# The order of exponentials and maxima in the fifteen sections with nine products: one order for both halves

## The chip, the cores and the metric

One core of a Trainium2 chip. The metric is device time in microseconds (us) of one execution, the median of three runs. The engines are called as in the profile: PE is TensorE (PEld its weight loads), DVE is VectorE, ACT is ScalarE, POOL is GpSimd, and SP issues most DMAs.

## The reference

```python
x = A_x                                                # 2048 x 512
g = _sigmoid((x * gate_w).sum(-1, keepdims=True))
a = einsum("ts,se->te", dft_seq_re, x @ dft_hid_re.T) - einsum("ts,se->te", dft_seq_im, x @ dft_hid_im.T)
qkv = x @ wqkv                                         # 32 heads of 16
p = softmax(q @ k.T * 16 ** -0.5)                      # for each head, 2048 x 2048
b = (p @ v, heads side by side) @ wo
out = g * a + (1 - g) * b
```

So there is an attention of 32 heads without a mask, and beside it a Fourier mixing by dense matrices; a gate mixes the two.

## The kernel before

Heads are taken in 16 pairs. A **unit** is one pair, one half of the queries (1024) and 128 keys; there are 512 units (`UNITS`). For each unit four score tiles of 128 keys x 512 queries are made: two query blocks `qb`, two heads `h`. Each is one matmul of 64 rows into one of seven PSUM banks (`scores`, L795), and one exponential on ACT that writes a quarter of the unit's tile `pt` (L796). Four `pt` tiles exist at a time. The softmax needs the maximum of each row ahead of the exponentials; for that the same products are made a second time with queries and keys exchanged, each reduced by a maximum on DVE (`a_tile`, L257 and L259), and the negated maximum goes into spare rows of the queries.

The **values** (`pv`, L831) multiply `pt` with the values of its 128 keys: for each unit four fp32 matmuls, j = 2 qb + h, each in 32 columns of the PE array of its own; the profile shows two records for each. Two units are added up in one bank, and ACT copies it (L840, or L837 for the first of a row of units); POOL adds the copies up (L846).

PE's array is split into two halves of 64 rows, so that two matmuls run side by side. What runs side by side is written out by hand as a **pattern** of slots. A letter is a score tile: "s" one that ends in an exponential, "a" one that ends in a maximum. A slot of one letter runs one dense product (`issue`, L472) on one half of the array beside a score on the other half. A slot of two letters runs two scores side by side, the first letter on the other half, the capital on the same half as the products. "d" is a dense product alone, "^" issues a small piece of deferred work of the maxima, and "|" ends the **segment**: what finishes a chain of products, the planned loads, then the values of the next two units. Scores come from two streams for each kind, one for each head h (`streams`); stream h lies on half h of the array. Segment `half` takes its products from half `half` of the array, its single letters from stream `1 - half`, its capitals from stream `half`.

A section is a pair of segments, half 0 and half 1, for the same products. Twelve sections (THIN) make the Fourier's first products, 96 (FULL) its second ones, one (EVEN) and then fifteen (TEN) the attention's output projection: nine products make one chain for 128 rows of the output, in the one bank `d`. The second half of a chain waits for the first score's reader after the last product of the segment before (`before`); the first half of the next one waits for the bank's reader, a scaling and adding on DVE (`finish`, L664), which is held back until the end of half 1 (`late`). Before all sections the routine `four` runs with four phases, and in each of them stream 0 is given one score tile ahead (`first_tiles`).

Which of the seven banks a tile gets is a plan: `bank()` takes the one that a small model of DVE's and ACT's queues (`read_by`: 2.6 slots a maximum, 2.1 an exponential) sees free first. PE, ACT, DVE and POOL each work through their instructions in the order of the program; semaphores hold what isn't ready.

Of the kernel before, what the change touches and what calls it, by code (L numbers as in the profile page):

```python
# [32 lines left out]
def mix_kernel(ctx: ExitStack, tc: tile.TileContext, xa_t, xa, wqkv, w_hid, w_seq, wo, gate_w, out):  # L33
# [821 lines left out]
    def take(gen, n, whole=True):  # L855

        got = []
        while len(got) < n:
            x = next(gen, None)
            if x is None:  # L860
                break
            x[0].left -= 1
            got.append((*x, x[0].left == 0))
            if whole and got[-1][4]:
                break
        return got
# [71 lines left out]
    FULL = "a s a s a s a s s a s a s a a s |"  # L938
    THIN = "aS s a s a s s a s a s a a sA |"
    EVEN = "aA s s a s ^ s d s sA a d sS |", "a s a sS a ^ s a s s s s a |"  # L940
    TEN = "aA s s a s ^ s s s a a sS |", "a s a sS a ^ s s s s s aA |"

    def stream(h):

# [74 lines left out]
    def pairs():  # L1019
# [3 lines left out]
        for i in range(2 * NT * 3):  # L1023
            yield (FULL,) * 2, take(seq, 16)
        for patterns, n in ((EVEN, 1), (TEN, 15)):
            for i in range(n):
# [83 lines left out]
```

## Time and profile before

| | |
|---|---|
| median of 3 runs | 1653.67 us (1653.55 to 1653.82) |
| the profiled execution | 1653.87 us, span 1651.8 us |
| PE, DVE, ACT, POOL busy | 99%, 82%, 77%, 46% of the span |
| the stretch of the fifteen sections, 1458.4 to 1601.5 us | ACT 137.41, DVE 108.04, POOL 46.86 of 143.10 us |
| one section | 8 + 8 exponentials, 2 copies, 10 maxima, 9 + 9 products |

The span goes from the first to the last instruction. A row of the timeline gives start and duration of consecutive instructions of one kind, their count, and in brackets the engine's idle time before them with what ended it. A row of the groups gives the count, the busy time, the mean of one in ns, and the idle time before them. PE's matmuls are pipelined: the duration of one is longer than its distance from the next.

### The profile page before, as it was taken

The page shows a single profiled execution, that of the slowest core. Times are in us where ns is not written, and L with a number is a line of the kernel's source. Part 1 is how long each engine was busy: PE and PEld are TensorE (multiplying, and loading weights), DVE is VectorE, ACT ScalarE, POOL GpSimd, SP SyncE. Part 2 cuts the span into 40 slices and gives each one's busy share as a digit, 9 for nine tenths or more (in the row PEclk, how much of TensorE's full clock was granted, in tenths as well). Part 3 has the DMA queues.
Part 4 walks back from the last instruction along what each step waited for, and adds up shares of the span by engine and source line. Part 5 has one row for each costly group of instructions (what it writes and reads, how often), then busy time and mean ns, then how long its engine had stood idle before and what let it go on. Part 6 is the DMA issues. An engine that isn't in the chain of part 4 may idle for free.

```text
span 1651.8 us, 35235 instructions
## 1 busy us (share of the span) xinstructions
PE 1643.1 (99%) x13169; PEld 1012.2 (61%) x13169; DVE 1356.4 (82%) x2285; ACT 1267.7 (77%) x2487; POOL 753.0 (46%) x813
## 2 busy tenths in 40 slices
PE   9999999999999999999999999999999999999998
PEld 7888866665555665565555555555555555555554
DVE  5469988888888888888888888888888888877776
ACT  5222178888888888888887888888888888899995
POOL 0124644554544555545454565554545566332341
PEclk9999999999999999999999999999999999999999
DMA  9953301112221234222227333322222333451114
GB/s 302 340 162 135 154 14 37 31 53 66 67 71 52 61 87 133 74 62 70 57 75 259 84 95 114 96 77 68 66 72 74 81 114 109 151 197 43 24 44 142
DMA packets 92481, 165.66 MB, mean 100 GB/s; under 512 B 23360, under 2 KB 24776, under 8 KB 91160
## 3 DMA queue, kind: packets, MB, share of 16 engines
q1 hardware_dynamic: 87672, 162.64, 32.2%
q8 instruction: 104, 1.70, 0.4%
q0 software_dynamic: 4352, 0.39, 0.2%
q14 instruction: 65, 0.53, 0.1%
q10 hardware_dynamic: 288, 0.39, 0.1%
HBM read 107.73 MB, written 54.52 MB: 98 GB/s over the span
## 4 chain that ended last, share of the span: by engine, by line
PE 99%; DVE 0%; DMA 0%; SPq 0%; DVEq 0%; ACT 0%; issue 0%
PE d L472 44%; PE t L831 28%; PE t L257 8%; PE t L795 6%; PE t L353 5%; PE t L92 2%; PE t L93 2%; PE t L91 2%; PE t L812 1%; PE t L472 1%; PE t L377 1%; DMA raw<-xa_t 0%; DVE mx L259 0%; DVE yp L664 0%; PE t L749 0%; PE t L727 0%
## 5 line engine op out<-in xcount | busy, mean ns | idle before, releaser
L259 DVE TENSOR_REDUCE mx<-t 128x1 f32<-128x512 f32 x2009 | 1232.6, 681 | 225.5 <-PE t L257 206.1
L796 ACT ACTIVATE pt<-t 128x512 f32<-128x512 f32 x2048 | 1031.1, 629 | 11.4 <-PE t L795 3.2
L257 PE MATMUL t<-ks,qs 64*128 64x512 f32 x2009 | 750.2, 407 | 0.1
L795 PE MATMUL t<-qs,ks 64*128 64x512 f32 x2048 | 729.2, 394 | 0.2
L472 PE MATMUL d<-xab,ch 64*128 64x512 f32 x2016 | 647.2, 396 | 0.0
L831 PE MATMUL t<-pt,vt 128*32 128x512 f32 x3968 | 477.2, 598 | 0.0
L472 PEld LDWEIGHTS d<-xab,ch 64*128 64x128 f32 x2016 | 366.9, 184 | 169.3 <-issue 99.7
L472 PE MATMUL d<-xab,cl 64*128 64x512 f32 x1008 | 399.2, 396 | 0.0
L257 PEld LDWEIGHTS t<-ks,qs 64*128 64x128 f32 x2009 | 357.8, 184 | 56.9 <-ACT pt L796 25.2
L795 PEld LDWEIGHTS t<-qs,ks 64*128 64x128 f32 x2048 | 367.9, 184 | 16.3 <-ACT pt L796 5.8
L846 POOL TENSOR_TENSOR osum<-osum,oe 128x512 f32<-128x512 f32 x217 | 279.1, 1286 | 157.6 <-ACT oe L840 155.8
L840 ACT COPY oe<-t 128x512 f32<-128x512 f32 x217 | 127.4, 587 | 187.2 <-PE t L831 179.0
L831 PEld LDWEIGHTS t<-pt,vt 128*32 128x32 f32 x3968 | 103.6, 109 | 223.8 <-issue 149.1
L472 PEld LDWEIGHTS d<-xab,cl 64*128 64x128 f32 x1008 | 185.8, 184 | 86.3 <-issue 49.4
L417 POOL CAST ch<-craw 128x512 fp32r<-128x512 f32 x126 | 77.2, 613 | 343.1 <-PE t L257 232.4
L418 POOL TENSOR_TENSOR cl<-craw,ch 128x512 fp32r<-128x512 f32 x126 | 162.1, 1286 | 10.2
L280 POOL DMA_DIRECT2D qs<-mt x132 | 73.5, 562 | 80.7 <-DVE mt L276 71.2
L472 PE MATMUL d<-wo_hl,o_hl 64*128 64x512 f32 x288 | 75.6, 395 | 0.0
L472 PE MATMUL d<-wre,xab 64*128 64x512 f32 x288 | 70.5, 390 | 0.0
L472 PEld LDWEIGHTS d<-wo_hl,o_hl 64*128 64x128 f32 x288 | 51.8, 184 | 18.5 <-ACT pt L796 13.4
L472 PEld LDWEIGHTS d<-wre,xab 64*128 64x128 f32 x288 | 52.8, 185 | 2.9
L92 PE MATMUL t<-xab,wh 128*128 128x512 f32 x124 | 48.4, 390 | 0.2 <-DVE xab L88 0.2
(123 smaller groups left out, 938.3 us busy)
## 6 DMA issues: line engine op xcount, KB each, us to landing
craw<-w_seq SPq DMA_DIRECT2D x128, 256.0 KB
qk<-hl SPq DMA_DIRECT2D x32, 512.0 KB
qs<-qk SPq DMA_DIRECT2D x84, 128.0 KB
ks<-qk SPq DMA_DIRECT2D x288, 32.0 KB
b<-hl SPq DMA_DIRECT2D x16, 512.0 KB
xab<-b SPq DMA_DIRECT2D x16, 512.0 KB
o<-osum SPq DMA_DIRECT2D x62, 128.0 KB
oh<-nh SPq DMA_DIRECT2D x12, 512.0 KB
```

Source lines behind the costliest of these rows:

```text
L92: nc.tensor.matmul(ps, sh, ml, start=False, stop=False)
L257: nc.tensor.matmul(ps, qs[p % 2][r, qt * P:(qt + 1) * P], ks[p % 2][r, kb * 512:(kb + 1) * 512], start=True, stop=True)
L259: user = nc.vector.tensor_reduce(mx[p % 2][:, h, qt, kb:kb + 1], ps, AX.X, ALU.max)
L353: i = nc.tensor.matmul(ps[c], st[r], mv[r], start=phase < 2 and j == 0, stop=phase > 1 and j == 11)
L417: nc.gpsimd.tensor_copy(h1, raw)
L418: nc.gpsimd.tensor_tensor(l1, raw, h1.bitcast(F32), ALU.subtract)
L472: i = nc.tensor.matmul(self.ps, st[r], mv[r], start=not self.begun, stop=stop)
L795: nc.tensor.matmul(ps, ks[p % 2][rr, kt * P:(kt + 1) * P], qs[p % 2][rr, q0:q0 + 512], start=True, stop=True)
L796: return nc.scalar.activation(pts[u][:, 2 * qb + h], ps, AF.Exp, bias=0.0, scale=DH ** -0.5)
L831: nc.tensor.matmul(acc[32 * j:32 * j + 32], vt[:, kt, p, h:h + 32], pt[:, j], start=u == us[0], stop=u == us[-1])
L840: nc.scalar.copy(oe, acc)
L846: nc.gpsimd.tensor_tensor(o, o, oe, ALU.add)
```

## The change

Both segments of the fifteen sections get the same pattern. It begins with a slot that pairs an exponential's tile with a maximum's, goes on with nine products beside s, a, s, a, s, s, a, s, a, and ends with two exponentials' tiles side by side. Each segment's count of each letter on each stream stays: seven s and four a from the far stream, one S and one A from the near one.

```diff
-    TEN = "aA s s a s ^ s s s a a sS |", "a s a sS a ^ s s s s s aA |"
+    TEN = ("sA s a s a ^ s s a s a sS |",) * 2
```

## The prediction

> **What bounds the kernel now.** I read the page first, then the granted clock and busy times of the stretch that the change touches, then that stretch's groups, then one section instruction by instruction.
>
> ```profile
> span 1651.8 us, 35235 instructions
> PE 1643.1 (99%) x13169; PEld 1012.2 (61%) x13169; DVE 1356.4 (82%) x2285; ACT 1267.7 (77%) x2487; POOL 753.0 (46%) x813
> ```
>
> By the page PE (TensorE) is the bound. That is an average, and a PE that holds a matmul in flight counts as busy. The fifteen sections with nine products lie between 1458.4 and 1601.5 us. The busy times of that stretch, and its groups:
>
> ```profile
> core 0: us, PE busy (x) PEld busy (x) DVE busy (x) ACT busy (x) POOL busy (x), PEclk, DMA share, GB/s
> 1458.40:1601.50 143.10, 143.10 (x1138) 78.84 (x1134) 108.04 (x177) 137.41 (x270) 46.86 (x48) 1.00 0.17 52
> ```
> ```profile
> L796 ACT ACTIVATE pt<-t 128x512 f32<-128x512 f32 x240 | 120.8, 628 | 0.8
> L840 ACT COPY oe<-t 128x512 f32<-128x512 f32 x27 | 15.8, 587 | 5.0 <-PE t L831 3.4
> ```
>
> Here ACT (ScalarE) works 137.41 of 143.10 us: 240 exponentials and 30 copies of the values' bank (27 of them in the second row). Nearly all its idle time, 5.0 us, stands before those copies. So ACT sets the pace, and the one thing it waits for is the end of the values' matmuls (L831). One section on ACT's timeline (start, duration, group, idle before):
>
> ```profile
> 1506.40 4.03 ACT L796 ACTIVATE pt<-t 128x512 f32<-128x512 f32 x8
> 1510.57 0.59 ACT L840 COPY oe<-t 128x512 f32<-128x512 f32 x1
> 1511.15 4.03 ACT L796 ACTIVATE pt<-t 128x512 f32<-128x512 f32 x8
> 1515.36 0.58 ACT L840 COPY oe<-t 128x512 f32<-128x512 f32 x1 [0.18 <-PE t L831]
> 1515.96 4.03 ACT L796 ACTIVATE pt<-t 128x512 f32<-128x512 f32 x8
> ```
>
> Eight exponentials, a copy, eight, a copy: half 0 then half 1. From 1506.40 to 1515.96 a section takes 9.56 us. The eight end 4.03 us after their start; their mean is 0.628, so they follow each other by (4.03 - 0.628) / 7 = 0.486. ACT then idles 1510.57 - 1510.43 = 0.14 us before the copy of half 0 and 1515.36 - 1515.18 = 0.18 before that of half 1. The loads of the values' weights and the first matmuls of each half show what PE does:
>
> ```profile
> 1505.59 0.50 PE L257 MATMUL t<-ks,qs 64*128 64x512 f32 x2
> ...
> 1508.52 0.16 PEld L831 LDWEIGHTS t<-pt,vt 128*32 128x32 f32 x8 [0.27 <-ACT pt L796]
> 1508.52 1.92 PE L831 MATMUL t<-pt,vt 128*32 128x512 f32 x16
> 1508.98 0.13 PEld L831 LDWEIGHTS t<-pt,vt 128*32 128x32 f32 x4 [0.30 <-issue]
> 1509.41 0.13 PEld L831 LDWEIGHTS t<-pt,vt 128*32 128x32 f32 x4 [0.30 <-issue]
> ...
> 1510.38 0.50 PE L257 MATMUL t<-ks,qs 64*128 64x512 f32 x1
> ...
> 1513.31 0.16 PEld L831 LDWEIGHTS t<-pt,vt 128*32 128x32 f32 x8 [0.25 <-ACT pt L796]
> 1513.77 0.13 PEld L831 LDWEIGHTS t<-pt,vt 128*32 128x32 f32 x4 [0.30 <-issue]
> 1514.20 0.13 PEld L831 LDWEIGHTS t<-pt,vt 128*32 128x32 f32 x4 [0.30 <-issue]
> 1515.17 0.50 PE L257 MATMUL t<-ks,qs 64*128 64x512 f32 x2
> ...
> 1515.51 0.38 PE L472 MATMUL d<-wo_hl,o_hl 64*128 64x512 f32 x1
> ```
>
> The values' sixteen instructions (eight matmuls, two records each) run in four waves of four, at 1508.52, 1508.98, 1509.41 and, one step of 0.43 later, 1509.84. Their start waits for an exponential. Which one can be worked out: the fourth of half 0 ends at 1506.40 + 3 x 0.486 + 0.628 = 1508.49, which is 0.03 before the waves; the fourth of half 1 ends at 1511.15 + 1.458 + 0.628 = 1513.24, 0.07 before them. So in both halves the values follow the **fourth** of eight exponentials, the last four run beside the waves, and the copy finds the waves only 0.14 to 0.18 us late.
>
> **The change part by part.** *Counts.* A half keeps 11 slots, 9 products, 8 exponentials and 5 maxima; each half still gives the far stream seven exponentials and four maxima and the near one one of each; "^" stays after the fifth slot. So streams, chains, plan and DMAs stand where they stood at every segment's end, and only the order inside a segment moves. Work added or removed: none, 0 us.
>
> *Which exponential the values need.* Counting `next()` on the streams: stream 0 was given four scores by the four row groups' phases before the sections, stream 1 none, and every section gives both eight. With V units valued, a section starts with stream 0 at 2V+4 tiles and stream 1 at 2V. Half 0 values units V and V+1, so it needs stream 1 up to 2V+4: its first four exponentials, now as before the first four on ACT. Half 1 values V+2 and V+3 and needs both streams up to 2V+8. Stream 0 stands at 2V+5 and brings three with its first three exponentials. Stream 1 got seven in half 0 and lacks one, unit V+3, query half 1, head 1. Only the capital S of half 1 brings it. Before, that S is in slot "sS", the fourth of half 1, and is the third of ACT's eight. After, it sits in the last slot and is **the eighth**. Its matmul is j = 3 of the second unit, the last of the values.
>
> *Price of that wait.* PE works in order through sixteen instructions; the first two waves can run early, but the third wave's last member waits for the eighth exponential, and its second record runs a wave later. From the third wave to the copy it is 1510.57 - 1509.41 = 1.16 us (1515.36 - 1514.20 gives 1.16 again), and a wave follows its exponential by 0.03 to 0.07. ACT, whose next instruction is that copy, then idles 1.19 to 1.23 us instead of 0.18: 1.01 to 1.05 more, taken as 1.03. Queued behind the waiting matmul on PE are all slots of the next half 0; behind the copy on ACT are that half's eight exponentials. Nothing covers it: ACT has no other work and its exponentials are the bound. 15 sections x 1.03 = 15.4 us. The cost can't be below nothing, since the eight exponentials were already done without a gap. If only the last record had to run after it, it would be one step of 0.43 less, 15 x 0.60 = 9.0; the two records per matmul speak for two waves, so I keep 15.4.
>
> The row shows eight weight loads at once, those of the second wave already beside the first wave's matmuls, so loads do run ahead of matmuls and one could hope that PE works past the waiting one. The Trainium skill, "TensorE: Matmul & The Clock Gate", section "The mechanism", says that matmuls start and end strictly in program order, and only weight loads are pulled ahead; by it nothing of the next half fills the gap and the sum stays, while a PE that worked past it would give about no loss. No run here shows that order at a wait in mid-group.
>
> *The first slot.* An exponential now comes at once instead of after a maximum's slot. ACT is at its copy then (1510.57 to 1511.15, first slot at 1510.38), so its next exponential starts no earlier: 0 us.
>
> *Maxima.*
>
> ```profile
> 1506.12 3.19 DVE L259 TENSOR_REDUCE mx<-t 128x1 f32<-128x512 f32 x5 [0.43 <-PE t L257]
> 1510.94 1.89 DVE L259 TENSOR_REDUCE mx<-t 128x1 f32<-128x512 f32 x3 [1.63 <-PE t L257]
> ...
> 1514.52 0.74 DVE L664 SCALAR_TENSOR_TENSOR yp<-d,omg,yp 128x512 f32<-128x512 f32 x1
> ```
>
> Five take 3.19 us, 0.64 each, beside eight exponentials of 4.03. Half 1 no longer ends in two maxima, so the finish of a chain (0.74) starts earlier on DVE: 0.5 + 3.19 + 0.74 = 4.4 us after the half's first matmul, before its eighth exponential ends (in half 0 that was 1510.43 - 1505.59 = 4.84 after it). The next half 0's first product waits on it through bank d and finds it done. Before, the finish was over at 1515.26 and the product started at 1515.51, so nothing is won either.
>
> *Banks.* Seven banks serve a segment's 13 tiles, so the values' bank is the seventh one that comes free. By the planner's costs (2.1 slots an exponential, 2.6 a maximum) it is the fourth exponential's in both orders. The last S takes the third maximum's. On the chip that maximum ends, in half 0, 0.53 (1506.12 - 1505.59) + 3 x 0.64 = 2.45 us after the first slot; the fourth exponential ends 1508.49 - 1505.59 = 2.90 after it. The cover is 0.45 less the slot of that S, about a quarter microsecond by PE's pace (11 slots from 1505.59 to the wait before 1508.52). So half 0 keeps its 0.14 us of idle: 0 us. If the cover failed, a values' start could be late by up to one maximum, 0.64.
>
> Sum: 1653.87 us (the profiled execution, span 1651.8 and 2.1 around it) + 15.4 = 1669.3; on the median of 1653.67, which is 0.2 lower, **1669.1 us**.
>
> **The rivals.**
>
> *All of the values wait.* Never before does an instruction inside the sixteen carry a wait of its own; if the wait came to stand at their head, four waves would follow the eighth exponential: 1510.57 - 1508.52 + 0.05 - 0.18 = 1.92 per section, 28.8 in all, 1682.5 us. For it: that the trace has no example of a wait in the middle. Against: the fourth exponential released the head until now, and the code asks for each quarter of the tile apart. 6%.
>
> *The maxima's banks.* If the third maximum came later than reckoned, half 0's values would start late too: between nothing and 15 x 0.64 = 9.6 more, up to 1678.7. It decides once that maximum ends 0.2 us later than above. Speaking for it: only 0.2 us of cover; against: DVE now gets its second maximum two slots after the first, in place of two in one slot, and is not behind. 7%.
>
> *Not slower: the late S isn't what ends the wait.* If the streams were one tile further ahead than I count, half 1's values would still need only the first four, and an order that feeds ACT from the first slot could at best remove the idle before the copies: 15 x (0.14 + 0.18) = 4.8 us, 1648.9. It decides if the third wave of half 1 starts before the eighth exponential ends. For it: the trace before can't tell data from bank, since the fourth exponential frees both. Against: the count, and that every older pattern has this S in the first four slots of half 1. 5%, of which 3% stays within 0.2%.
>
> *The clock.* PE will stand still for about 1 us in each section. A gap that dropped the granted clock would stretch PE's 4.6 us (1505.59 to 1510.44 less a wait of 0.27) of the next half. At half speed that is 4.6 us more, of which the wait of 0.3 takes up a part: 4.3 in each of 15 sections, beside what is forecast, 1734 us.
>
> ```profile
> 1642.50:1646.50 4.00, 2.23 (x18) 1.06 (x16) 3.28 (x9) 1.52 (x3) 2.48 (x3) 1.00 0.34 133
> ```
>
> In the last microseconds PE works 2.23 of 4.00 us, and the clock granted is 1.00. 2%. The Trainium skill, same page, section "A second HAM failure mode: psum-queue depth-cycling", says that short idle times between groups of matmuls that cycle through banks can make the gate swing between half and full clock; by it this would be the outcome, and the row just quoted shows none of it.
>
> **How the numbers follow.** Forecast 80%, rivals 6, 7, 5 and 2%. The range takes the bounds of the unknown costs: below, a single wave behind the late exponential, 1653.67 + 9.0 = 1662.7; above, half a maximum's delay in half 0, 1669.1 + 15 x 0.32 = 1673.9. That is 1662.7 to 1673.9, and leaves out some 15%. A measurement of this kernel can tell about 0.2%, 3.3 us: faster 2%, same 3%, slower 95%.
>
> **What would show it right or wrong.** Right: on ACT's timeline every second copy has an idle time of about 1.2 us before it, released by L831, and the others keep about 0.14; sections last 10.6 us; the values' loads of half 1 show a wait on an exponential in their middle, with two waves after it; the group L840 has about 20 us of idle time instead of 5.0; the clock in the stretch is 1.00. Wrong: both copies of a section late (banks), an idle time of 2.1 us (all values wait), 0.7 us (one wave), or no more than 0.18.

## The result, and the profile after

The changed kernel takes 1667.7 us (median of 5, 1667.55 to 1667.81) against 1653.82 of the kernel before on the same chip: a ratio of 1.0083, interval 1.0071 to 1.0094, or 13.9 us slower. The profiled execution's span is 1665.7 us, 13.9 more than before. The prediction said 1669.1 us (1662.7 to 1673.9), slower, with 80% on a late capital S in half 1.

The page's head, and the busy times of the stretch with the fifteen sections (this window runs to the end of the last copy, 157.7 us; the one of before, 143.1 us, ended about 1 us ahead of it):

```profile
span 1665.7 us, 35222 instructions
...
1458.60:1616.30 157.70, 157.70 (x1144) 83.87 (x1142) 106.46 (x179) 135.51 (x271) 47.77 (x52) 1.00 0.16 47
```

The engines do the same work as before, the granted clock (the last but two) is 1.00, and ACT's share of the stretch has fallen from 96 to 86%. ACT's timeline for one section, with the copy before it:

```profile
1510.71 0.59 ACT L840 COPY oe<-t 128x512 f32<-128x512 f32 x1 [1.19 <-PE t L831]
1511.19 4.03 ACT L796 ACTIVATE pt<-t 128x512 f32<-128x512 f32 x8
1515.53 0.59 ACT L840 COPY oe<-t 128x512 f32<-128x512 f32 x1 [0.30 <-PE t L831]
1516.01 4.03 ACT L796 ACTIVATE pt<-t 128x512 f32<-128x512 f32 x8
1521.23 0.58 ACT L840 COPY oe<-t 128x512 f32<-128x512 f32 x1 [1.19 <-PE t L831]
1521.71 0.61 ACT L796 ACTIVATE pt<-t 128x512 f32<-128x512 f32 x1
```

A section has grown from 9.56 to 1521.71 - 1511.19 = 10.52 us. Before every copy that ends half 1, ACT idles 1.19 us in place of 0.18; all fifteen rows of this kind say 1.19. The loads of the values' weights and PE's matmuls around them show why:

```profile
1510.55 0.50 PE L795 MATMUL t<-qs,ks 64*128 64x512 f32 x1
...
1513.02 0.53 PE L795 MATMUL t<-qs,ks 64*128 64x512 f32 x2
1513.48 0.16 PEld L831 LDWEIGHTS t<-pt,vt 128*32 128x32 f32 x8 [0.24 <-ACT pt L796]
...
1515.33 0.50 PE L795 MATMUL t<-qs,ks 64*128 64x512 f32 x1
...
1517.82 0.53 PE L795 MATMUL t<-qs,ks 64*128 64x512 f32 x2
1518.27 0.16 PEld L831 LDWEIGHTS t<-pt,vt 128*32 128x32 f32 x8 [0.25 <-ACT pt L796]
1518.73 0.12 PEld L831 LDWEIGHTS t<-pt,vt 128*32 128x32 f32 x3 [0.30 <-issue]
1519.16 0.12 PEld L831 LDWEIGHTS t<-pt,vt 128*32 128x32 f32 x3 [0.31 <-issue]
1520.09 0.14 PEld L831 LDWEIGHTS t<-pt,vt 128*32 128x32 f32 x2 [0.81 <-ACT pt L796]
1521.07 0.49 PE L795 MATMUL t<-qs,ks 64*128 64x512 f32 x1
```

In half 1 the values' sixteen records no longer run as four waves of four. Eight loads, then three, then three: fourteen records run on time. The last two, both of the fourth quarter of the second unit, wait until 1520.09. The eighth exponential ends at 1516.01 + 4.03 = 1520.04. The next half starts 0.98 later.

Half 0, from its first slot to the next half's, takes 1515.33 - 1510.55 = 4.78 us (before 4.79). Half 1 takes 1521.07 - 1515.33 = 5.74 (before 4.79). The loss is in half 1, 0.95 a section. Added up from copy to copy, from the last one ahead of the sections to the last one in them, the stretch was 1602.04 - 1457.88 = 144.16 us and is 1615.82 - 1458.17 = 157.65: 13.5 us more, and the other 0.4 of the 13.9 lie outside the sections. Eleven sections lose 0.95 on average. The three with a copy L837 lose 0.83, as they were a little longer before (9.64 in place of 9.56). The last loses 0.54: in the kernel before, its copy of half 0 was once 0.57 late in place of 0.14 (the row below), and after the change it is as late as the others, 0.30.

```profile
1597.27 0.59 ACT L840 COPY oe<-t 128x512 f32<-128x512 f32 x1 [0.57 <-PE t L831]
```

### The profile page after: what moved, and what is told of

Read it like the earlier page. It is cut to its first block, busy times and chain, and to the rows that moved or that the text cites. A ratio compares the mean times of both kernels' runs of the same rounds, so it can differ in the third digit from the quotient of the medians.

```text
span 1665.7 us, 35222 instructions
## 1 busy us (share of the span) xinstructions
PE 1656.9 (99%) x13169; PEld 1016.3 (61%) x13169; DVE 1353.8 (81%) x2285; ACT 1264.8 (76%) x2487; POOL 752.8 (45%) x813
## 4 chain that ended last, share of the span: by engine, by line
PE 99%; DVE 0%; DMA 0%; DVEq 0%; SPq 0%; issue 0%
PE d L472 43%; PE t L831 28%; PE t L257 8%; PE t L795 7%; PE t L353 5%; PE t L93 2%; PE t L92 2%; PE t L91 2%; PE t L812 1%; PE t L472 1%; PE t L377 1%; DVE mx L259 0%; DMA raw<-wqkv 0%; PE t L192 0%; DVE yp L664 0%; PE t L749 0%
## 5 line engine op out<-in xcount | busy, mean ns | idle before, releaser
L257 PE MATMUL t<-ks,qs 64*128 64x512 f32 x2009 | 761.4, 404 | 0.1
L795 PE MATMUL t<-qs,ks 64*128 64x512 f32 x2048 | 744.2, 396 | 0.2
L831 PE MATMUL t<-pt,vt 128*32 128x512 f32 x3968 | 491.2, 598 | 0.0
L257 PEld LDWEIGHTS t<-ks,qs 64*128 64x128 f32 x2009 | 362.2, 184 | 42.5 <-ACT pt L796 10.2
L472 PE MATMUL d<-wo_hl,o_hl 64*128 64x512 f32 x288 | 71.6, 389 | 0.0
```

The source lines that it names most:

```text
L257: nc.tensor.matmul(ps, qs[p % 2][r, qt * P:(qt + 1) * P], ks[p % 2][r, kb * 512:(kb + 1) * 512], start=True, stop=True)
L472: i = nc.tensor.matmul(self.ps, st[r], mv[r], start=not self.begun, stop=stop)
L795: nc.tensor.matmul(ps, ks[p % 2][rr, kt * P:(kt + 1) * P], qs[p % 2][rr, q0:q0 + 512], start=True, stop=True)
L831: nc.tensor.matmul(acc[32 * j:32 * j + 32], vt[:, kt, p, h:h + 32], pt[:, j], start=u == us[0], stop=u == us[-1])
```

## The experiments

Theory: the values of half 1 need the tile that the capital S brings; the change makes it the eighth exponential, and the last quarter of the values with its two records waits for it. Rival one: the mixed order of exponentials and maxima costs something by itself. Rival two: the hand-over from ACT to PE has a fixed price, or the whole block of values waits. "Slower" and "faster" below are against runs of the kernel before on the same chip.

**The late S in the old order.**

```diff
-    "a s a sS a ^ s s s s s aA |"
+    "a s a sA a ^ s s s s s aS |"
```

> The old patterns with one swap in half 1: the capital S of the fourth slot and the capital A of the last slot change places, so that only the late S is new. Theory (the values of half 1 wait for this S, now the eighth exponential): exponentials start 0.6 us after the copy as before, so the eighth ends 4.8 us after the half's first slot; 0.05 and two waves (0.98) behind it the next half begins, 5.84 in place of 4.79. 15 x 1.05 = 15.7 us slower than before, about 1.5 us slower than the change itself, whose exponentials start 0.1 earlier. Rival (the mixed order of the two kinds costs, not the S): the old order is kept, so within 2 us of before.

Measured: 1668.89 us against 1653.91, ratio 1.009 (1.0075 to 1.0105), 15.0 us slower. One exchange of two capitals makes all of the loss. It makes 1.1 us more than the change; the two intervals overlap, but the rows show where that comes from. ACT's rows for the end of half 1, half 0 and the end of the next half 1:

```profile
1510.71 0.59 ACT L840 COPY oe<-t 128x512 f32<-128x512 f32 x1 [1.19 <-PE t L831]
1511.33 4.03 ACT L796 ACTIVATE pt<-t 128x512 f32<-128x512 f32 x8
1515.50 0.59 ACT L840 COPY oe<-t 128x512 f32<-128x512 f32 x1
1516.09 4.03 ACT L796 ACTIVATE pt<-t 128x512 f32<-128x512 f32 x8
1521.30 0.58 ACT L840 COPY oe<-t 128x512 f32<-128x512 f32 x1 [1.19 <-PE t L831]
```

The idle time is the same 1.19. The exponentials start 0.59 to 0.62 us after the start of their copy, where the change has 0.48: that is its small gain, 0.1 a half, and half 1 keeps it.

**Half 0 alone.** TEN is the new pattern for half 0 and the old one for half 1.

> The new pattern in half 0 alone, half 1 as before. Theory: half 0 was 4.79 us and is 4.78 in the changed kernel, and half 1 gets its S early again: within 1 us of before. Rival (the mixed order costs): half of the loss, some 7 us.

Measured: 1653.77 against 1653.91, ratio 0.9999 (0.999 to 1.0009). The new order in half 0 costs nothing and brings nothing.

**The same order, one tile of lead.**

```diff
-    EVEN = ..., "a s a sS a ^ s a s s s s a |"
+    EVEN = ..., "a s a sS a ^ s a s s s s aS |"
```

> The changed kernel, with the same order of slots in all fifteen sections, but stream 1 is given one score tile ahead: the last slot of the section before them, a single a that has no product left, becomes aS. The late S then belongs to a unit that is valued a segment later. Theory: the loss goes although the order stays; both halves take 4.78 us, within 1.5 us of before. Rival (the mixed order costs): the loss stays, 14 us. Rival (any late exponential is waited for, by whatever rule): the loss stays too.

Measured: 1653.81 against 1653.91, ratio 1.0 (0.999 to 1.0009). The order of the slots in the fifteen sections is that of the change to the letter; only which unit's tile the late S brings is another. The loss is gone, so it is a wait for data and not the order. Both copies of a section now find the values 0.28 late:

```profile
1506.40 0.58 ACT L840 COPY oe<-t 128x512 f32<-128x512 f32 x1 [0.28 <-PE t L831]
1506.89 4.03 ACT L796 ACTIVATE pt<-t 128x512 f32<-128x512 f32 x8
1511.20 0.59 ACT L840 COPY oe<-t 128x512 f32<-128x512 f32 x1 [0.28 <-PE t L831]
1511.68 4.03 ACT L796 ACTIVATE pt<-t 128x512 f32<-128x512 f32 x8
1515.99 0.59 ACT L840 COPY oe<-t 128x512 f32<-128x512 f32 x1 [0.28 <-PE t L831]
1516.47 4.04 ACT L796 ACTIVATE pt<-t 128x512 f32<-128x512 f32 x8
```

**The S as the sixth and as the seventh exponential.** Half 1 is "sA s a s a ^ s sS a s a s |" or "sA s a s a ^ s s a sS a s |".

> The changed kernel with half 1's double slot sS moved up, so that the S is the sixth exponential and not the eighth. Theory: the sixth ends 0.68 + 5 x 0.486 + 0.628 = 3.74 us after the first slot, and the fourth matmul of the second unit would start at 2.93 + 0.86 = 3.79 anyway, so nothing waits: within 1.5 us of before. Rival (the wait stands ahead of all the values): the values would start at 3.79 in place of 2.93, 0.86 x 15 = 13 us slower than before.

> The changed kernel with half 1's double slot sS two slots earlier than the end, so that the S is the seventh exponential. Theory: the seventh ends 0.486 before the eighth, and each quarter waits by itself, so of the loss of 0.95 a section 0.48 is left: 7 us slower than before. Rival (late at all or not, by the end of the segment): 14 us, or none.

Measured: the sixth 1654.81 against 1653.91, ratio 1.0005 (0.9996 to 1.0014); the seventh 1659.97 against 1654.07, ratio 1.0034 (1.0021 to 1.0048), 5.9 us and not quite 7. With the eighth at 13.9 us this is a price with a threshold: the fourth quarter of the second unit has its own time to start, and an exponential costs only what it ends beyond that. In the run with the seventh:

```profile
1505.89 0.16 PEld L831 LDWEIGHTS t<-pt,vt 128*32 128x32 f32 x8 [0.28 <-ACT pt L796]
1506.35 0.12 PEld L831 LDWEIGHTS t<-pt,vt 128*32 128x32 f32 x3 [0.30 <-issue]
1506.78 0.12 PEld L831 LDWEIGHTS t<-pt,vt 128*32 128x32 f32 x3 [0.31 <-issue]
1507.19 0.14 PEld L831 LDWEIGHTS t<-pt,vt 128*32 128x32 f32 x2 [0.29 <-ACT pt L796]
```

An idle time of about 0.3 stands before every group of loads. The late S shows in the last two, which come 1507.19 - 1505.89 = 1.30 us after the first eight, and 1520.09 - 1518.27 = 1.82 in the change.

**The S second, the A last.** Half 1 is "sS s a s a ^ s s a s a sA |".

> The changed kernel with half 1's capitals exchanged: sS first, sA last. The S is early again, and DVE's first maximum comes two slots later. Theory (banks): the values' start is 0.46 us after the last slot, and the last slot waits for the sixth bank of the half to come free; with maxima that end at 1.7, 2.3 and 2.9 us after the first slot and exponentials at 1.3, 1.8, 2.3 and 2.8, that is 2.8 in place of 2.45, so half 1 takes 5.1 and not 4.79: 15 x 0.3 = 5 us slower than before. Rival (only the place of the S counts): within 1 us of before.

Measured: 1657.96 against 1654.07, ratio 1.0023 (1.0014 to 1.0033), 3.9 us slower. No load inside the values waits for a late exponential any more, but the last slot of half 1 comes later. The rows show the half's first slot, its last one and the head of the values:

```profile
1501.65 0.29 PEld L795 LDWEIGHTS t<-qs,ks 64*128 64x128 f32 x3 [0.84 <-issue]
...
1504.45 0.18 PEld L257 LDWEIGHTS t<-ks,qs 64*128 64x128 f32 x1 [0.16 <-ACT pt L796]
1504.88 0.16 PEld L831 LDWEIGHTS t<-pt,vt 128*32 128x32 f32 x8 [0.24 <-DVE mx L259]
```

From the first slot to the last it is 1504.45 - 1501.65 = 2.80 us, as reckoned, where the change has 1517.82 - 1515.33 = 2.49. The 0.24 before the values is no delay: the run without copies, below, has the same 0.24 there with nothing waited for. So an early S alone doesn't bring the old time back; which kind stands in the first slot of half 1 is worth 3.9 / 15 = 0.26 us a section. That this goes through the banks that the maxima free is the reckoning; the times fit it, and no run separates it from other causes.

**The values backwards.** In the fifteen sections `pv` goes through its eight matmuls in the opposite order.

> The changed kernel, in its fifteen sections with the values' eight matmuls in the opposite order, so that the quarter written by the late S is the first and not the last. The same sums in another order. Theory: in half 1 all four waves then stand behind the eighth exponential, two more than in the changed kernel: 15 x 0.86 = 13 us slower than it, 27 slower than before; half 0 as it was. Rival (the price is a fixed delay of the hand-over between ACT and PE): no slower than the changed kernel.

Measured: 1864.35 against 1654.07, ratio 1.1266 (1.1249 to 1.1284). The edit also put the plan of banks wrong in every section, so this time doesn't answer the question. The next run has the same order of the values with the plan left alone:

> The run before with the opposite order of the values, with the plan of banks left alone: its edit reused the variable that tells the plan which bank the values take, so that the plan was wrong in all sections, and its time says nothing of the order. Theory as there: all four waves of half 1 behind the eighth exponential, 15 x 0.86 = 13 us slower than the changed kernel, 27 slower than before. Rival (a fixed delay of the hand-over): no slower than the changed kernel.

Measured: 1694.05 against 1653.91, ratio 1.0246 (1.0229 to 1.0263): 40 us slower and not 27. Two ends of half 1:

```profile
1519.80 0.59 ACT L843 COPY oe<-t 128x512 f32<-128x512 f32 x1 [2.10 <-PE t L832]
...
1532.67 0.59 ACT L843 COPY oe<-t 128x512 f32<-128x512 f32 x1 [3.57 <-PE t L832]
```

In seven of the fifteen sections the copy waits 2.10 us, which is about 1.19 and two waves of 0.43 more, as expected. In the other eight it waits 2.93 to 3.59. The values' matmuls at both places, and the granted clock (the third number from the end), first at the first place and then at the second:

```profile
1517.75 1.92 PE L832 MATMUL t<-pt,vt 128*32 128x512 f32 x16 [1.76 <-ACT pt L796]
...
1529.15 3.41 PE L832 MATMUL t<-pt,vt 128*32 128x512 f32 x16 [1.76 <-ACT pt L796]
```
```profile
1518.00:1520.00 2.00, 2.00 (x20) 0.61 (x14) 0.00 (x0) 0.20 (x1) 0.00 (x0) 1.00 0.00 0
...
1528.00:1529.00 1.00, 0.00 (x0) 0.00 (x0) 0.70 (x2) 1.00 (x3) 0.00 (x0) 1.00 0.00 0
1529.00:1530.00 1.00, 0.85 (x8) 0.38 (x12) 0.00 (x0) 0.10 (x1) 0.00 (x0) 0.72 0.00 0
1530.00:1531.00 1.00, 1.00 (x9) 0.22 (x4) 0.00 (x0) 0.00 (x0) 0.00 (x0) 0.50 0.00 0
1531.00:1532.00 1.00, 1.00 (x8) 0.00 (x0) 0.00 (x0) 0.00 (x0) 0.00 (x0) 0.50 0.00 0
```

At both places PE stood still for 1.76 us; right after the second the clock fell to half, and after the first it stayed at 1.00. The eight sections with the long waits are exactly those in which it fell. So 15 x 0.86 = 13 us of the loss over the change are the two waves, and the rest goes with the clock.

**Without most of the copies.** The kernel with one tile of lead, and in the sections

```diff
+        if us[0] >= UNITS - 76 and kt < NT - 1:
+            return
         oe = work.tile([P, 512], F32, name="oe", bufs=2)
```

> The kernel with one tile of lead (order of the change, nothing late), without ACT's copies of the values' bank and POOL's adds in the fifteen sections, except for the first and the last two units of each row of sixteen: the sums over keys lack those parts. ACT has 0.48 us less to do in nearly each half. The prediction's reading (ACT sets the pace): every such half gets shorter, as far as PE lets it. Rival (PE's own path of slots, change-over and waves sets it, 2.41 + 0.46 + 1.86 = 4.73 of 4.79): less than 2 us faster, and ACT's idle time grows by what was taken away.

Measured: 1653.55 against 1654.07, ratio 0.9997 (0.9987 to 1.0006). ACT has a tenth less to do and nothing gets shorter. Its exponentials, and the head of the values in one half:

```profile
1501.76 4.03 ACT L796 ACTIVATE pt<-t 128x512 f32<-128x512 f32 x8 [0.77 <-PE t L257]
1506.54 4.03 ACT L796 ACTIVATE pt<-t 128x512 f32<-128x512 f32 x8 [0.76 <-PE t L257]
1511.33 4.03 ACT L796 ACTIVATE pt<-t 128x512 f32<-128x512 f32 x8 [0.76 <-PE t L257]
```
```profile
1508.94 0.16 PEld L831 LDWEIGHTS t<-pt,vt 128*32 128x32 f32 x8 [0.24 <-issue]
```

Two halves are 9.57 us (before 9.56), and the idle time is 0.76 before each eight: ACT waits for PE's tiles.

## Why the prediction was right, and where its steps were not

*The count of the streams and the late S: right.* The wait stands where it was put, in the middle of half 1's values and on the last matmul; it goes with one tile of lead and comes with one exchange of capitals.

*The price of the wait: right.* 1.19 us of idle time were measured where 1.19 to 1.23 were reckoned, and two records ran behind it. The other places of the S fit: next to nothing at the sixth (0.9 us, with no change inside its interval), 5.9 us at the seventh, and two waves more when the quarter comes first.

*The first slot, taken at 0 us: mis-sized by 0.09 a section.* With a score in the first slot the exponentials start 0.48 after the copy (1511.19 - 1510.71) and not 0.58 to 0.61. The eighth ends 1520.04 - 1515.33 = 4.71 after the half's first slot; before it was 1515.18 - 1510.38 = 4.80. So 1.03 a section became 0.95, and with the three sections of 0.83 and the last of 0.54 the sections lost 13.5 us in place of the 15.4 of the sum. The old order with a late S, which lacks this gain, lost 15.0.

*"ACT sets the pace", and the fourth exponential as what starts the values: wrong.* The last slots of the kernel before, and DVE's maxima of half 0 after the change:

```profile
1508.04 0.52 PE L795 MATMUL t<-qs,ks 64*128 64x512 f32 x2
...
1512.86 0.53 PE L257 MATMUL t<-ks,qs 64*128 64x512 f32 x2
```
```profile
1511.12 3.08 DVE L259 TENSOR_REDUCE mx<-t 128x1 f32<-128x512 f32 x5 [2.00 <-PE t L257]
```

With exponentials that start earlier, half 0's values start at 1513.48, and the fourth exponential ended at 1511.19 + 3 x 0.486 + 0.628 = 1513.28. They follow the last slot (1513.02) by 0.46, as they did before (1508.04 to 1508.52, or 1512.86 to 1513.31). By the times, in half 0 that slot's S follows the bank of the third maximum, which ends 1511.12 - 1510.55 + 3 x 0.62 = 2.43 us after the first slot (the last slot starts 2.47 after it); but PE's own slots, one each 0.23 us, come out there at much the same time, and no run tells the two apart. From there PE's own path runs to the next half: 0.46 and the waves. So half 0 kept 4.78 us, and what the earlier exponentials won was lost again: its copy's idle time grew from 0.14 to 0.30, where the prediction's sign was that it keeps about 0.14. The prediction had found both bounds, a quarter of a microsecond apart, and held them apart by a slot of 0.23; the way from the last slot to the values is twice that. The run without copies shows that ACT is not the bound in the new order with a tile of lead. For the kernel before this is argued: its sections take the same time, and exponentials that start earlier gained nothing in half 0. The forecast came out because the new wait is longer than all of this: once ACT's eighth exponential holds the values' end, ACT's chain is what counts in half 1, as was assumed.

*PE standing still for about 1 us: wrong.* The prediction let two waves run ahead of the late exponential. In fact fourteen of the sixteen records do. The loads run one wave ahead, so the third wave's three records start at about 1519.16 and three second records one step of 0.43 later, at 1519.59. With 0.59 us for one record these end at 1520.18, after the late quarter's start at 1520.09:

```profile
1518.27 2.87 PE L831 MATMUL t<-pt,vt 128*32 128x512 f32 x16
```

So PE's records leave no gap: the row has no idle time in it, and in the stretch PE is busy for 157.70 of 157.70 us. The granted clock stayed at 1.00, and since the gap on which the clock's rival rested did not come, the change didn't put that rival to the test. The Trainium skill, "TensorE: Matmul & The Clock Gate", section "The mechanism", has matmuls start strictly in program order: taken matmul by matmul the trace agrees, no slot of the next half starts before the late matmul (1521.07 after 1520.09), and what ran ahead are, by the counts of three, the second records of matmuls that come before it.

## What to carry to other kernels

Where a hand-written order feeds several streams into one consumer, write down for each consumer which items it needs and at which place of the producer's queue each of them ends; the capital S's early place in half 1 looked like an accident of taste and was what mattered most in that line (15.0 us for its exchange with the A in the old order, against 3.9 for having the A last in the new one). A late item costs only what it ends beyond the time at which its part of the consumer would have started, so the item that the consumer uses last can come latest. An engine that is 96% busy is not for that reason the bound: take some of its work away and see whether anything moves.

## What the runs showed of the hardware that was not expected

In the run with the values backwards and the plan left alone, PE's matmuls stood still for 1.70 to 1.76 us ahead of the values of half 1 in all fifteen sections. After eight of these gaps the granted clock fell to 0.50, and at the place shown the values' four waves took 3.41 us in place of 1.92. After the other seven, just as long, it stayed at 1.00. So the length of the gap alone doesn't decide. In the trace's record of the clock each of the eight falls lasts 3.41 us, and their starts lie 4, 7, 7, 4, 7, 7 and 14 times 3.41 us apart. They came 0.3 to 0.95 us after the end of their gap; after the other seven gaps the next point of that grid was 0.9 to 3.2 us away. Where the gap lies on this grid goes with the fall, in one execution with fifteen gaps; no run shows why. In the changed kernel, whose records leave no gap, the clock stayed at 1.00.

The Trainium skill, "TensorE: Matmul & The Clock Gate", section "A second HAM failure mode: psum-queue depth-cycling", describes such swings from short pauses between groups of matmuls. The trace of this run agrees in kind, with eight falls to 0.50; the prediction gave such a fall 2% for the change, and it did not come there.
